# W1 in two pieces behind its first three groups, and new engine orders for the middle blocks

## The chip, the cores and the metric

The kernel runs on one core of one Trainium2 chip. The metric is the device time of one execution in microseconds (us). The time before is the median of three runs, 292.15 us (291.99 to 292.51).

## The reference, cut to what matters

All inputs are float32. Eight batches of eight heads, 576 rows, head width 64; then 4608 tokens of width 512 through a two-layer network with 2048 hidden columns.

```python
def _attn_ref(q, k, v):
    q_s = np.exp(q - np.max(q, axis=-1, keepdims=True))
    q_s = q_s / (np.sum(q_s, axis=-1, keepdims=True) + 1e-09)
    k_s = np.exp(k - np.max(k, axis=2, keepdims=True))
    k_s = k_s / (np.sum(k_s, axis=2, keepdims=True) + 1e-09)
    kv = np.einsum('bhsd,bhse->bhde', k_s, v)
    return np.einsum('bhsd,bhde->bhse', q_s, kv)

def _moe_ref(x, w_in, w_out):
    h = x @ w_in
    g = np.where(h > 0.0, h, np.exp(np.minimum(h, 0.0)) - 1.0)
    return g @ w_out
# x is the attention's result, transposed to tokens x 512
```

## The kernel before, in words

**Tiles.** The network runs over nine blocks of 512 tokens, called j = 0 to 8. In a block the 2048 hidden columns are eight groups g = 0 to 7 of 256 columns. A group takes eight matmuls of 128x512 on PE (`hg_mm`, L622) into one PSUM buffer of 1024 columns. ACT takes the exponential (L672), for most groups ACT then takes 1 minus it, cut at zero (L674), and DVE joins both with the product into the tile GR (L678, two halves). Only when DVE has read the buffer may PE use it again, which is two groups later. The second layer is `out_mm` (L699) for blocks 0 and 1. From block 2 on it is `pair` (L832), seven products in the place of eight; these need sums of parts of GR (`add_sum`, L783, on DVE or POOL) and of parts of the weights W2 (`combos`, L759), and DVE adds up the results (L841).

**Attention beside it.** Sixteen half batches n = 0 to 15 are worked on between the groups of earlier blocks. Each loads Q, K and V (L361), takes exponentials on ACT (L397, L401), row sums on DVE (L423, L425), scales Q (L435, on DVE or POOL) and casts V (L279). From n = 4 on a DMA transpose on SP's queue (L472) turns the scaled Q into QT, and `widen` (L279) copies it to qsT. PE takes K times V (L509); DVE makes MBLK out of it (L518, L522); PE multiplies with qsT (L540), and `xt` copies the result into XT (L279), the input of the first layer.

**Order.** Nothing is scheduled at run time. `program` adds some 1400 operations, numbered in the order in which they are added; `ORDER` lists, for each of the five engines, which of them it runs and in which order. An operation with several possible engines (`alts`) goes to the one whose list holds its number. `emit` puts a semaphore wait ahead of an operation where something that it needs runs on another engine or is a DMA. Each engine works through its list in order, and so an operation that waits holds up all that stand behind it on its engine. `AFTER` adds four waits by hand.

**Loads of W1.** POOL issues them (`load_w1`, L379). Columns of groups 0 to 2 come first in four parts (operations 14 to 17, 384 KB each), then group 3, group 4, group 5 (18, 19, 20; 512 KB each), then groups 6 and 7 (21; 1024 KB). POOL's list begins `1 32 14 15 24 16 17 18 48 40 19 20 21 69 68 70`: 48 scales Q, 40 casts V, both for half batch 1, and 69, 68 and 70 are loads of W2 and Q. PE reaches groups 3, 4, 5, 7, 6 of block 0 in this order (operations 99, 103, 110, 133, 121). The wait for a load stands ahead of a group's first weight load (PEld).

**Operations named below**, by their numbers of before:

- 318: scaling of Q for n = 7 (L435). 355: copy of a finished output tile (L279). 241: a copy into XT (L279). 360 (ACT, L674), 361 and 362 (DVE, L678): block 2, group 3. 370: first layer of block 2, group 5, which waits for 362; ahead of it on PE stands 313 (L540).
- 671 (DVE, L841) and 672 (PE, L832): one partial result in block 3's second layer.
- 564 and 565 (ACT), 566 and 567 (DVE): block 3, group 7 with its first-layer product 563. 579 (DVE, L678): block 4, group 0, second half; 645: first layer of block 4, group 2, which waits for 579.
- 219, 230, 236: loads of K (n = 6), Q and V (n = 7) on SP's queue. 180, 181, 183, 184, 186, 187, 189, 190: the eight stores of block 0 (L728). 238: the cast of V on POOL that waits for load 236. 393: a sum of W2 parts on POOL. 240: PE's products that wait for 238 (L540, L509).

Of the kernel before, what the change touches and what calls it, by code (L numbers as in the profile page):

```python
# [24 lines left out]
ISSUE = {"sp": 550, "act": 550, "gp": 740}  # L25
ORDER = {
# [24 lines left out]
    "act": (  # L51
# [12 lines left out]
    "dve": (  # L64
# [37 lines left out]
}  # L102

APART = ((1, 1), (1, 2))
AFTER = ((209, 197), (228, 261), (235, 275), (307, 288))


class Op:
    __slots__ = ("eng", "dur", "emit", "deps", "key", "idx", "start", "end",
# [167 lines left out]
class Gen:  # L277
# [610 lines left out]
    def program(self):  # L888
# [8 lines left out]
        self.load_w1(0, 3, (0,), -30, [gate])  # L897
        for kc in range(1, 4):
            self.load_w1(0, 3, (kc,), -30)
        for g0, g1 in ((3, 4), (4, 5), (5, 6), (6, 8)):  # L900
            self.load_w1(g0, g1, range(4), -30)
        AB, C, D_ = 3, 2, 1
        self.stage1(0, -8, vconv=CAST0)
# [174 lines left out]
            one[i]()  # L1078
            two[i]()
        for a, b in AFTER:  # L1080
            S.ops[a].deps.setdefault(S.ops[b], "raw")


S_ = S
# [32 lines left out]
```

## Time and profile before

| | us |
|---|---|
| median of three runs (lowest, highest) | 292.15 (291.99, 292.51) |
| time of the profiled execution | 292.0 |
| its span in the trace | 290.2 |
| time outside of the span | 1.8 |
| busy: PE, DVE, ACT, POOL | 280.1, 231.5, 212.1, 160.3 |
| DMA, mean over the span | 172 GB/s |

The span runs from the first to the last instruction that the trace holds. Busy times are sums over instructions; matmuls overlap, and so a busy PE need not be a PE without gaps. The chain of waits is followed back from the last instruction, and where the chain stays on PE, PE had work at hand.

### The profile page before, as it was taken

What the parts mean: (1) busy time and instruction counts of PE and PEld (TensorE: products, weight loads), DVE (VectorE), ACT (ScalarE), POOL (GpSimd) and SP (SyncE); (2) the same over time, 40 slices, a digit from 0 to 9 for tenths busy, and PEclk for the clock granted to TensorE, in tenths of its full rate; (3) what the DMA queues carried; (4) which work ended last, traced back from release to release, by engine and by line L of the source; (5) the groups of instructions that cost most, each with busy time, mean ns of one, the idle gap of its engine ahead of it and who ended that gap; (6) DMA issues with size and microseconds to landing.
All of it is one profiled execution on the core that took longest, in us unless ns stands there. A gap on an engine that the chain in (4) does not pass through costs nothing.

```text
span 290.2 us, 5483 instructions
## 1 busy us (share of the span) xinstructions
PE 280.1 (97%) x2176; PEld 243.7 (84%) x2176; DVE 231.5 (80%) x432; ACT 212.1 (73%) x237; POOL 160.3 (55%) x159
## 2 busy tenths in 40 slices
PE   2899999999999999999999999999999999999995
PEld 0488887888888899989899998989999999989995
DVE  3758847886699998898998879797785978668884
ACT  4858838989999877989887788857687546655510
POOL 1992443426356679409776793845417712794441
PEclk9999999999999999999999999999999999999999
DMA  7999999897989724775686457322211001400244
GB/s 260 395 369 388 390 388 357 219 212 253 267 246 292 209 103 111 248 189 172 133 267 198 122 82 277 69 48 52 63 36 38 0 2 30 114 0 20 56 97 123
DMA packets 36474, 50.04 MB, mean 172 GB/s; under 512 B 16352, under 2 KB 18144, under 8 KB 36448
## 3 DMA queue, kind: packets, MB, share of 16 engines
q1 hardware_dynamic: 29680, 33.96, 42.6%
q0 software_dynamic: 6528, 15.47, 17.6%
q8 instruction: 17, 0.28, 0.4%
q10 hardware_dynamic: 240, 0.26, 0.3%
q14 instruction: 9, 0.07, 0.1%
HBM read 36.70 MB, written 9.44 MB: 159 GB/s over the span
## 4 chain that ended last, share of the span: by engine, by line
PE 91%; DVE 3%; DMA 2%; POOL 2%; ACT 0%; SPq 0%; issue 0%
PE PS L622 44%; PE PS L832 32%; PE PS L699 9%; PE PS L540 3%; DMA KR<-in_k_dram 2%; PE PS L509 2%; DVE GR L678 1%; POOL W L379 1%; DVE QS L435 0%; DVE ZQ L423 0%; POOL VB L279 0%; PE PS L459 0%; POOL QS L435 0%; DVE MBLK L522 0%; ACT GE L674 0%; SPq L361 0%
## 5 line engine op out<-in xcount | busy, mean ns | idle before, releaser
L622 PE MATMUL PS<-XT,W 128*128 128x512 f32 x576 | 141.5, 393 | 0.1
L622 PEld LDWEIGHTS PS<-XT,W 128*128 128x128 f32 x576 | 105.3, 188 | 21.1 <-DVE GR L678 0.3
L678 DVE SCALAR_TENSOR_TENSOR GR<-PS,GE 128x512 fp32r<-128x512 f32 x112 | 76.7, 686 | 20.6 <-ACT GE L674 19.2
L672 ACT ACTIVATE GE<-PS 128x1024 f32<-128x1024 f32 x56 | 57.4, 1024 | 43.1 <-PE PS L622 36.2
L783 POOL TENSOR_TENSOR GR<-GR 128x256 fp32r<-128x256 f32 (+1 forms) x50 | 48.5, 981 | 47.7 <-DVE SB L783 29.0
L674 ACT ACTIVATE GE<-GE 128x1024 f32<-128x1024 f32 x56 | 59.4, 1060 | 1.5
L832 PE MATMUL PS<-TB,GR 128*128 128x256 f32 x336 | 52.5, 283 | 0.0
L832 PE MATMUL PS<-W,GR 128*128 128x256 f32 x336 | 52.2, 283 | 0.0
L832 PEld LDWEIGHTS PS<-TB,GR 128*128 128x128 f32 x336 | 46.5, 191 | 1.4 <-DVE OSB L841 0.3
L832 PEld LDWEIGHTS PS<-W,GR 128*128 128x128 f32 x336 | 46.5, 191 | 1.1
L435 POOL TENSOR_TENSOR QS<-QR,RZQ 128x1152 f16<-128x1152 f32 (+1 forms) x15 | 27.7, 1845 | 29.5 <-DVE RZQ L425 26.2
L841 DVE TENSOR_TENSOR OSB<-OSB,PS 128x256 f32<-128x256 f32 x84 | 34.8, 416 | 10.8 <-PE PS L832 9.3
L699 PE MATMUL PS<-W,GR 128*128 128x512 f32 x128 | 32.2, 394 | 0.0
L783 POOL TENSOR_TENSOR GR<-SB,GR 128x256 fp32r<-128x256 f32 (+1 forms) x26 | 25.4, 985 | 8.2 <-PE PS L832 7.4
L699 PEld LDWEIGHTS PS<-W,GR 128*128 128x128 f32 x128 | 23.6, 188 | 4.5
L423 DVE TENSOR_REDUCE ZQ<-QR 128x18 f32<-128x1152 f32 (+2 forms) x18 | 21.7, 1208 | 5.8 <-ACT QR L421 4.9
L783 POOL TENSOR_TENSOR SB<-GR 128x256 fp32r<-128x256 f32 (+1 forms) x19 | 18.6, 981 | 11.8 <-PE PS L832 7.1
L401 ACT ACTIVATE KR<-KR 128x1152 bf16<-128x1152 f32 x16 | 18.4, 1158 | 2.7 <-DMA KR<-in_k_dram 2.7
L783 DVE TENSOR_TENSOR GR<-GR 128x256 fp32r<-128x256 f32 (+1 forms) x34 | 19.9, 595 | 0.1
L397 ACT ACTIVATE QR<-QR 128x1152 f32<-128x1152 f32 x14 | 16.2, 1158 | 1.8 <-DMA QR<-in_q_dram 1.7
L279 POOL CAST VB<-VR 128x1152 bf16<-128x1152 f32 (+1 forms) x11 | 12.2, 1111 | 8.6 <-DMA VR<-in_v_dram 8.6
L832 PE MATMUL PS<-W,SB 128*128 128x256 f32 x104 | 16.8, 283 | 0.0
(67 smaller groups left out, 265.1 us busy)
## 6 DMA issues: line engine op xcount, KB each, us to landing
out_dram<-OSB SPq DMA_DIRECT2D x61, 128.0 KB, 2.4
QR<-in_q_dram SPq DMA_DIRECT2D x12, 576.0 KB, 5.4
KR<-in_k_dram SPq DMA_DIRECT2D x12, 576.0 KB, 5.4
VR<-in_v_dram SPq DMA_DIRECT2D x12, 576.0 KB, 5.7
W<-in_moe_w_out_dram POOLq DMA_DIRECT2D x4, 1024.0 KB, 16.3
QR<-in_q_dram POOLq DMA_DIRECT2D x4, 576.0 KB, 11.9
VR<-in_v_dram POOLq DMA_DIRECT2D x4, 576.0 KB, 13.0
KR<-in_k_dram POOLq DMA_DIRECT2D x4, 576.0 KB, 14.0
```

The source lines that it names most:

```text
L397: S.add("act", t_act(1152, False), lambda e: e.activation(flat(q), flat(q), AF.Exp), key - 3, X=[f"qR{i}0", f"qR{i}1"])
L401: S.add("act", t_act(1152, False), lambda e: e.activation(ek[:, :, :, :].rearrange("p h c d -> p (h c d)"), flat(k), AF.Exp), key - 2, X=[ ...
L423: S.add("dve", t_dve(m), lambda e, qp=qp, zp=zp: e.tensor_reduce(zp, qp, AX.X, ALU.add), key - 3, R=[f"qR{i}{x}" for x in xs], W=[f"ZQ{i}{ ...
L435: lambda e, qp=q[:, :, a:b, :], rz=rz, dst=qs[:, :, a:b, :]: e.tensor_tensor(dst, qp, rz, ALU.mult),
L622: last = e.matmul(P[:, t * 512:(t + 1) * 512], self.W1[:, kc, tt * 128:(tt + 1) * 128], self.XT[:, kc, rc:rc + BLK], start=(kc == 0), stop ...
L672: S.add("act", t_act(1024, True), lambda e: e.activation(ge, P, AF.Exp), key, W=own, X=banks)
L674: S.add("act", t_act(1024, False), lambda e: e.activation(ge, ge, AF.Relu, bias=1.0, scale=-1.0), key, X=own)
L678: S.add("dve", t_dve(512 if j else 1024), lambda e, u=u: e.scalar_tensor_tensor(*(x[:, :, u, :] if j else x for x in (gt, P)), 0.0, ge[:, ...
L699: last = e.matmul(dst, self.tile(jb, jj, ts), self.W2[:, jj, c0:c1], start=(jj == 0), stop=(jj == 15))
L783: lambda e: e.tensor_tensor(dst, a, b, op), key, R=R, W=W, X=X, after=after)
L832: last = e.matmul(dst, a[i][:, y_, :], b[i][:, y_, :], start=start and i == 0 and y_ == 0, stop=stop and i == len(grps) - 1 and y_ == z - ...
L841: S.add("dve", t_dve(256), lambda e: e.tensor_tensor(dst, a, b, ALU.add), key, R=R, W=W, X=X, after=after)
```

## The change

The loads of W1 behind the first three groups become two: groups 3 and 4 (1024 KB), and groups 5 to 7 (1536 KB). There are two operations fewer, and so every number from 22 on is two lower in the lists of after. The lists of all five engines are given anew. Apart from the two loads that are gone and from SP's stores (below), they differ from the last second-layer products of block 1 (about 69 us in the trace of before) to the middle of block 6 (about 212 us), and neither ahead of that nor behind it. `AFTER` names the same four pairs of operations under their new numbers, and writes the wait in where `setdefault` left one of another kind as it was; none of the four pairs had one.

```diff
-        for g0, g1 in ((3, 4), (4, 5), (5, 6), (6, 8)):
+        for g0, g1 in ((3, 5), (5, 8)):
             self.load_w1(g0, g1, range(4), -30)
...
-AFTER = ((209, 197), (228, 261), (235, 275), (307, 288))
+AFTER = ((207, 195), (226, 259), (233, 273), (305, 286))
...
         for a, b in AFTER:
-            S.ops[a].deps.setdefault(S.ops[b], "raw")
+            S.ops[a].deps[S.ops[b]] = "raw"
...
     "gp": (
-        "1 32 14 15 24 16 17 18 48 40 19 20 21 69 68 70 73 72 71 74 75 76 77 120 131 116 143 144 "
+        "1 30 14 15 22 16 17 18 46 38 19 67 66 68 71 70 69 72 73 74 75 118 129 114 141 142 161 130 "
...
     "sp": (
-        "8 9 10 11 12 13 205 207 210 220 229 219 180 230 236 309 308 190 183 356 184 347 239 181 "
-        "249 357 189 319 187 248 326 186 348 320 418 392 377 391 329 378 338 419 494 495 511 510 "
+        "8 9 10 11 12 13 203 205 208 218 227 185 187 181 179 217 178 188 228 182 234 307 306 355 "
+        "184 237 354 345 247 317 324 346 246 376 318 389 416 390 375 336 327 417 492 493 337 427 "
...
     "dve": (
-        "275 276 222 282 283 305 288 306 289 295 296 355 302 303 316 343 242 344 243 317 244 318 "
-        "245 352 246 353 247 415 361 362 394 395 416 314 367 368 405 373 323 374 376 402 407 403 "
+        "273 274 220 280 281 303 304 286 287 293 294 300 301 314 315 239 240 341 342 241 242 243 "
+        "413 350 244 245 351 359 414 360 403 365 366 374 393 371 372 405 400 406 397 380 381 460 "
...
-        "582 552 536 537 556 562 568 539 540 545 628 541 546 630 572 566 567 616 617 621 442 443 "
-        "592 578 444 579 654 655 445 650 637 446 638 593 659 665 447 671 648 649 642 747 675 697 "
+        "543 566 544 538 539 570 564 590 439 615 626 440 630 565 441 442 576 652 577 653 443 629 "
+        "444 591 635 657 445 636 663 646 669 745 647 673 586 667 588 695 668 679 696 694 680 746 "
```

Read with the numbers of before, the new lists do this:

- 73 operations change their engine: 24 go from DVE to POOL (19 sums of GR, 4 sums of W2, the scaling 318), 19 sums of GR from POOL to DVE, 14 copies from DVE to ACT (355 among them), 6 copies from ACT to DVE (241 among them), 8 copies and casts from ACT to POOL, 2 casts from POOL to ACT. PE's 457 operations, DMAs left aside, stay the same.
- SP issues 187, 189, 183 and 181 right behind the transpose 229 and ahead of load 219, 190 ahead of load 230, and 184 ahead of load 236 (180 stood ahead of 230 before).
- POOL runs 393 ahead of 238; before, it ran 238 first.
- DVE's list from 566 to 579 is 566, 592, 441, 617, 628, 442, 632, 567, 443, 444, 578, 654, 579. ACT's list has 564 right behind 433, with no exponential of K (437) between.

125 rows, old and new, of the table ORDER are left out of this document.

## The prediction

> **What bounds the kernel now.** I read first the span and PE's clock, then busy times, then what PE waited for, then the chain of waits.
>
> ```profile
> core 0: 290.2 us, clock 0.999
> PE 280.1 (97%) x2176; PEld 243.7 (84%) x2176; DVE 231.5 (80%) x432; ACT 212.1 (73%) x237; POOL 160.3 (55%) x159
> PE PS L918 <- ACT QR L421: 5.7, 1, 5.7
> ```
>
> The third row is the longest of PE's waits by far, and it is the start: PE waits for the first Q. The chain, in order of time, shows the rest.
>
> ```profile
> 14.44 1.58 PE PS L622 x6
> ...
> 16.49 13.20 PE PS L622 x58
> ...
> 75.75 0.20 PE PS L540 x2
> ...
> 76.87 0.49 ACT XT L279
> ...
> 80.48 1.37 DVE QS L435
> ...
> 83.77 1.35 DVE ZQ L423
> ...
> 85.88 0.70 DVE GR L678
> ...
> 86.63 2.08 PE PS L622 x8
> ...
> 125.40 1.66 PE PS L832 x14
> ...
> 135.00 1.84 PE PS L622 x8
> ...
> 271.46 15.37 PE PS L832 x128
> 286.85 0.42 DVE OSB L841
> ```
>
> From 14.44 us PE carries the chain to 286.85, but for one stretch from 76.87 to 86.63. Between lies PE's own work at full clock: 272.4 us. Neither its 457 operations nor the lists ahead of 69 us (PE's) and behind 212 us change. The change can take away only what PE waits between 14.4 and 286.9, and that is little; it can add as much as the new lists hold PE up. So there is much more room above the time than below it.
>
> The one stretch off PE, closer (instructions in order of time):
>
> ```profile
> 83.42 1.06 ACT L674 ACTIVATE GE<-GE 128x1024 f32<-128x1024 f32 x1
> ...
> 86.13 0.40 PE L540 MATMUL PS<-qsT,MBLK 128*128 128x256 f32 x2
> ...
> 86.63 1.66 PEld L622 LDWEIGHTS PS<-XT,W 128*128 128x128 f32 x8 [0.31 <-DVE GR L678]
> ```
>
> PE's weight load for 370 stood idle for 0.31 us until DVE had read the buffer (362, the chain's 85.88 row). That is what the new lists can win here: 0.3 us. The short gaps at changes between kinds of product stay, since their products do.
>
> **The change part by part.** *The wait at 86.3 us.* 361 could have started when ACT's 360 ended, 83.42 + 1.06 = 84.48. It started only behind a row sum that ended at 83.77 + 1.35 = 85.12. Ahead of it DVE loses 318 (1.37) and the copy 355 (512 columns, priced at the 0.69 of L678's 512, row below), and gains 241 (384 columns, under 0.69; I take 0.5): 1.5 us less. So 361 starts at 84.5. With a reciprocal now between, at half of 0.69, 362 ends at 84.5 + 0.69 + 0.35 + 0.69 = 86.2, and PE comes to 370 at 86.63 - 0.31 = 86.3. The wait goes, by a hair: -0.3 us. POOL takes 318 and ACT takes 355; POOL has 45% of the span free, and ACT loses 241 (0.49) to DVE just there.
>
> *W1 in two pieces.* The POOL issues, their way to landing, the weight loads on PE and the rate of all DMAs:
>
> ```profile
> 10.87 1.39 POOL L379 DMA_DIRECT2D W<-in_moe_w_in_dram  x2
> ...
> 13.71 0.82 POOL L379 DMA_DIRECT2D W<-in_moe_w_in_dram  x1
> ...
> 14.52 1.47 POOL L379 DMA_DIRECT2D W<-in_moe_w_in_dram  x2
> ...
> W<-in_moe_w_in_dram POOLq DMA_DIRECT2D x1, 384.0 KB, 5.6
> ...
> W<-in_moe_w_in_dram POOLq DMA_DIRECT2D x1, 512.0 KB, 6.7
> ...
> W<-in_moe_w_in_dram POOLq DMA_DIRECT2D x1, 1024.0 KB, 9.4
> ...
> 20.23 0.19 PEld L622 LDWEIGHTS PS<-XT,W 128*128 128x128 f32 x1
> ...
> 23.63 0.41 PEld L622 LDWEIGHTS PS<-XT,W 128*128 128x128 f32 x2
> ...
> 11.50:15.00 3.50, 2.69 (x48) 1.46 (x47) 2.52 (x9) 2.65 (x4) 3.50 (x6) 1.00 1.22 402
> 15.00:20.00 5.00, 5.00 (x23) 4.07 (x22) 1.54 (x3) 2.21 (x3) 5.00 (x8) 1.00 1.69 358
> 20.00:25.00 5.00, 5.00 (x24) 4.13 (x23) 4.58 (x6) 4.67 (x6) 3.43 (x5) 1.00 1.42 385
> ```
>
> The last of the four early parts is issued at 10.87 and lands 5.6 later, at 16.5. Group 4's piece (13.71 + 6.7) lands at 20.4, groups 6 and 7 (issued in the last row at 14.52 + 0.73 = 15.25, + 9.4) at 24.6. PE's first weight load of group 3 is at 20.23, that of group 5 two groups later at 23.63 + 0.22 = 23.85. Now group 3 must wait for what was group 4's landing, and group 5 for what was that of groups 6 and 7. The DMA engines are never idle here (last figure of the windows, GB/s): 402 where rows of 3 KB come in, 358 with 1 KB rows, 385 with 2 KB rows. The new pieces have 2 KB and 3 KB rows. The first, 1.05 MB, gains 2.93 - 2.72 = 0.2 and lands at 20.2, in time within 0.1. The second, 1.57 MB at 402, takes 3.9 and lands at 24.1: PE stops for group 5 for 24.1 - 23.85 = 0.25, with the semaphore 0.3 us. Bounds: with the bytes no faster than now it lands at 24.6, 0.8 us; with the rate steady from 16.5 on (2.62 MB in 6.6 us, 23.1), 0. I take +0.3. Behind 30 us no PE wait of the trace could swallow it. POOL's two issues fewer (0.74 each) start the loads behind them 1.5 us earlier; since the engines are full this gives those loads the 0.5 us that the rates give, and no product waits for them: 0.
>
> [...]
>
> *The other lists.* 73 operations change engine. Prices:
>
> ```profile
> L678 DVE SCALAR_TENSOR_TENSOR GR<-PS,GE 128x512 fp32r<-128x512 f32 x112 | 76.7, 686 | 20.6 <-ACT GE L674 19.2
> ...
> L672 ACT ACTIVATE GE<-PS 128x1024 f32<-128x1024 f32 x56 | 57.4, 1024 | 43.1 <-PE PS L622 36.2 <-PE PS L832 6.8
> ...
> L783 POOL TENSOR_TENSOR GR<-GR 128x256 fp32r<-128x256 f32 x33 | 26.1, 796 | 29.8 <-DVE SB L783 20.0 <-PE PS L832 9.6
> ...
> L783 DVE TENSOR_TENSOR GR<-GR 128x256 fp32r<-128x256 f32 x23 | 12.5, 554 | 0.1
> ```
>
> A sum of 256 columns costs POOL 0.80 and DVE 0.55. Five operations more leave DVE for POOL than come back, 14 copies go to ACT and 6 come: DVE becomes shorter, and most new places have room. I followed the lists; DVE is closest to PE at 645, which waits for 579. PE leaves 563 at about 125.4 + 0.1; ACT's 564 and 565 (1.02 + 1.06) follow at once and end at 127.6. Then DVE has 13 operations: four halves of L678 (2.74), a row sum (1.35), a sum of 512 columns (628, as 0.69), two of 256 (617 and 632, 1.1) and the copy 441 (0.55), together 6.4; and four short ones, between nothing and 0.55 each. It ends between 134.0 and 136.2, and PE begins 645 at 135.0. So between no wait and 1.2 us; the middle, 135.1, costs 0.1, which I take.
>
> *SP's stores* wait for nothing new, but stand ahead of three loads (rivals). The new `AFTER` puts in the same four waits: 0.
>
> The sum goes against the profiled execution: 290.2 of span and 1.8 outside of it, 292.0, which is 0.15 below the median of 292.15 and inside the three runs. 292.0 - 0.3 + 0.3 + 0.1 = **292.1 us**. This is no change: I count under 0.2% (0.6 us), about the spread of the three runs, as what a measurement can't tell from none.
>
> **The rivals.** *All waits go (faster).* W1's second piece lands at 23.1 to 23.8, 645 finds 579 done, 370's wait goes: 292.0 - 0.3 = 291.7. POOL's issue ahead of PE's start may be shorter with 2 KB rows (0.82 for a lone one of 1 KB rows against 1.47 / 2 for the last two), 0.1, and some tenths of shorter waits inside PE's stretches may go as well: 291.4. For it: longer rows move faster in the windows. Against: group 4's landing at 20.4, 3.9 us behind the early parts for 1.05 MB that take 2.9 at 358; this 1 us of lag the new pieces inherit.
>
> *A V load late (slower).* SP's queue, the landing of load 236 in its window, and POOL:
>
> ```profile
> 62.08 1.31 SPq L361 DMA_DIRECT2D KR<-in_k_dram  x1
> 63.44 0.55 SPq L728 DMA_DIRECT2D out_dram<-OSBX  x1
> ...
> 65.39 0.37 SPq L361 DMA_DIRECT2D VR<-in_v_dram  x1
> ...
> VR<-in_v_dram SPq DMA_DIRECT2D x1, 576.0 KB, 5.9
> ...
> 68.31 2.12 POOL L435 TENSOR_TENSOR QS<-QR,RZQ 128x1152 f16<-128x1152 f32 x1 [0.90 <-DVE RZQ L425]
> 71.37 1.15 POOL L279 CAST VB<-VR 128x1152 bf16<-128x1152 f32 x1 [0.94 <-DMA VR<-in_v_dram]
> ...
> 82.80 2.41 POOL L759 TENSOR_TENSOR TB<-W 128x1024 fp32r<-128x1024 f32 x1
> ```
>
> Six stores more stand between the transpose and load 236: at 0.6 each 3.6 us of issue, of which 0.8 was free; it goes out 2.8 later, at 68.2, and lands at 74.1 in the place of 71.3. POOL now runs 393 (2.41) first, to 72.9, waits, and ends the cast at 74.1 + 1.15 = 75.25; PE wants it at 75.75. From a landing at 74.6 on each us later stops PE, and with it the cast's followers on POOL. If the stores' own 0.8 MB slow the queue by another 1 to 1.5 us, PE loses 0.5 to 1.0: 292.6 to 293.1, say 292.9.
>
> *DVE and POOL in each other's way (slower).* 0.55 is the mean of DVE's sums beside a busy POOL. If POOL's added work makes DVE's four operations in SBUF ahead of 579 (592, 617, 628, 632) longer by 0.25 each, 645 waits 1.0 more: 293.1. For it: the lists put POOL's longest sums where DVE is full. Against: DVE also loses work. [...]
>
> *The lists don't do it.* 370's wait stays, since the reciprocal and ACT's new copy use up the hair: 292.4, no change.
>
> **How the numbers follow.** Forecast 0.38 (291.6 to 292.7, same); all waits go 0.23, of it 0.17 beyond 0.2% and 0.06 within; V load 0.15 and DVE against POOL 0.18, both slower; the lists don't do it 0.06, same. Faster 0.17, same 0.38 + 0.06 + 0.06 = 0.50, slower 0.33. The range for 8 in 10 takes in the faster case down to 291.4 and the slower ones up to 293.2.
>
> **What would show it.** Right: the chain from 14.4 us is all PE, without the ACT and DVE rows between 77 and 86; the weight load of group 5 in block 0 comes at 24.1 to 24.2 with an idle time for a DMA of W; cast 238 ends ahead of 75.6; PE's last row starts where now 286.85 stands, within 0.3. Wrong: an idle PE weight load for VB near 76 (V load), or for GR near 105, 135 or 142 (DVE); or no idle time at 24 us at all.

## The result and the profile after

| | before | after |
|---|---|---|
| median of eight executions each (us) | 292.31 | 293.46 |
| lowest, highest (us) | 291.99, 293.06 | 292.83, 294.87 |
| profiled execution, its span (us) | 292.0, 290.2 | 294.87, 293.1 |

The changed kernel is slower by 0.4%, 1.2 us: ratio 1.0041, 95% interval 1.0021 to 1.0061. The prediction had 292.1 us and a range up to 293.2. The profiled execution of after is the longest of its eight, so its waits are at their long end; the experiments below say what each costs at the median.

The span, the busy times and what PE and its weight load waited for, in the trace of after (waits: us in total, times, longest; those that before has too, or that lie ahead of PE's steady run at 14 us, are left out):

```profile
core 0: 293.1 us, clock 0.999
```
```profile
PE 280.6 (96%) x2176; PEld 243.4 (83%) x2176; DVE 228.4 (78%) x419; ACT 209.6 (72%) x239; POOL 173.4 (59%) x168
```
```profile
PE PS L621 <- DVE GR L677: 1.0, 1, 1.0
PE PS L539 <- POOL VB L278: 0.9, 1, 0.9
...
PE PS L621 <- DMA W<-in_moe_w_in_dram: 0.5, 1, 0.5
...
PEld PS L539 <- POOL VB L278: 1.3, 1, 1.3
...
PEld PS L621 <- DVE GR L677: 1.2, 1, 1.2
...
PEld PS L621 <- DMA W<-in_moe_w_in_dram: 0.9, 1, 0.9
```

PE's busy time is that of before within 0.5 us. Three waits are new: 2.4 us by PE's rows, 3.4 by those of its weight load, which runs ahead of PE (a product begins 0.12 us behind the start of its weight load, median in after). Less the 0.3 us of the wait that went, these are 2.1 and 3.1 us; the 2.9 us by which the span grew lie between the two. The chain of waits has the same three places, where before it had only the stretch from 76.87 to 86.63:

```profile
13.65 11.14 DMA W<-in_moe_w_in_dram
24.83 5.76 PE PS L621 x24
...
69.61 6.73 DMA VR<-in_v_dram
76.40 1.16 POOL VB L278
...
198.31 2.31 DVE SB L782
200.65 0.70 DVE GR L677
201.37 0.70 DVE GR L677
202.12 2.11 PE PS L621 x8
...
274.33 15.36 PE PS L831 x128
```

Between 78 and 192 us all its pieces are PE's. The last row started at 271.46 before: 2.87 us late. In time order (timeline of after):

```profile
24.83 0.76 PEld L621 LDWEIGHTS PS<-XT,W 128*128 128x128 f32 x4 [0.93 <-DMA W<-in_moe_w_in_dram]
...
61.14 2.38 SPq L471 DMA_TRANSPOSE QT<-QS  x1
63.56 2.95 SPq L727 DMA_DIRECT2D out_dram<-OSBX  x4
66.55 0.60 SPq L360 DMA_DIRECT2D KR<-in_k_dram  x1
67.19 1.14 SPq L727 DMA_DIRECT2D out_dram<-OSBX  x2
68.37 0.59 SPq L360 DMA_DIRECT2D QR<-in_q_dram  x1
69.00 0.57 SPq L727 DMA_DIRECT2D out_dram<-OSBX  x1
69.61 0.59 SPq L360 DMA_DIRECT2D VR<-in_v_dram  x1
...
76.40 1.15 POOL L278 CAST VB<-VR 128x1152 bf16<-128x1152 f32 x1 [2.82 <-DMA VR<-in_v_dram]
...
77.60 0.30 PEld L539 LDWEIGHTS PS<-qsT,MBLK 128*128 128x128 f32 x2 [1.35 <-POOL VB L278]
...
88.37 1.01 PEld L621 LDWEIGHTS PS<-XT,W 128*128 128x128 f32 x5
...
198.20 2.13 POOL L434 TENSOR_TENSOR QS<-QR,RZQ 128x1152 f16<-128x1152 f32 x1
...
198.31 2.31 DVE L782 TENSOR_TENSOR SB<-GR 128x256 fp32r<-128x256 f32 x1
...
200.65 1.42 DVE L677 SCALAR_TENSOR_TENSOR GR<-PS,GE 128x512 fp32r<-128x512 f32 x2
...
202.12 1.69 PEld L621 LDWEIGHTS PS<-XT,W 128*128 128x128 f32 x8 [1.17 <-DVE GR L677]
```

Three stories. At 24 us the second W1 piece is late. At 77 us the load of V goes out behind seven stores (at 65.39 before), lands at 69.61 + 6.73 = 76.34, and PE waits for its cast. At 202 us PE waits for DVE, whose sum of 256 columns took 2.31 us: it began 0.11 us behind a POOL instruction and ended 0.29 us behind that one's end (198.20 + 2.13 = 200.33). The weight load at 88.37 has no idle time: the wait of before at 86.63 is gone.

### The profile page after: what moved, and what is told of

Same layout as the page of the kernel before. It is cut to its first block, busy times and chain, and to the rows that moved or that the text cites. A ratio compares the mean times of both kernels' runs of the same rounds, so it can differ in the third digit from the quotient of the medians.

```text
span 293.1 us, 5465 instructions
## 1 busy us (share of the span) xinstructions
PE 280.6 (96%) x2176; PEld 243.4 (83%) x2176; DVE 228.4 (78%) x419; ACT 209.6 (72%) x239; POOL 173.4 (59%) x168
## 4 chain that ended last, share of the span: by engine, by line
PE 84%; DMA 8%; DVE 3%; POOL 2%; ACT 1%; issue 0%; SPq 0%
PE PS L621 40%; PE PS L831 30%; PE PS L698 9%; DMA W<-in_moe_w_in_dram 4%; PE PS L539 3%; DMA VR<-in_v_dram 2%; DMA KR<-in_k_dram 2%; PE PS L508 2%; POOL W L378 1%; DVE GR L677 1%; DVE SB L782 1%; POOL VB L278 1%; DVE OSB L840 0%; PE PS L458 0%; POOL QS L434 0%; ACT GE L673 0%
## 5 line engine op out<-in xcount | busy, mean ns | idle before, releaser
L782 POOL TENSOR_TENSOR GR<-GR 128x256 fp32r<-128x256 f32 (+1 forms) x47 | 45.1, 968 | 35.5 <-DVE SB L782 25.3
L434 POOL TENSOR_TENSOR QS<-QR,RZQ 128x1152 f16<-128x1152 f32 (+1 forms) x16 | 30.6, 1910 | 23.5 <-DVE RZQ L424 21.4
L782 POOL TENSOR_TENSOR GR<-SB,GR 128x256 fp32r<-128x256 f32 (+1 forms) x26 | 24.5, 948 | 18.1 <-DVE GR L782 9.0
L782 POOL TENSOR_TENSOR SB<-GR 128x256 fp32r<-128x256 f32 (+1 forms) x22 | 21.4, 977 | 7.5 <-DVE GR L677 6.5
L782 DVE TENSOR_TENSOR GR<-GR 128x256 fp32r<-128x256 f32 (+1 forms) x37 | 21.3, 587 | 0.1
L278 ACT ACTIVATE OSB<-PS 128x256 f32<-128x256 f32 (+1 forms) x24 | 9.7, 407 | 15.4 <-PE PS L831 14.2
L278 ACT ACTIVATE XT<-PS 128x640 fp32r<-128x640 f32 (+6 forms) x22 | 12.8, 586 | 6.8 <-PE PS L539 3.7
L671 ACT ACTIVATE ESB<-PS 128x1024 f32<-128x1024 f32 x14 | 14.1, 1026 | 4.5 <-PE PS L621 4.1
```

The costliest lines, as they stand in the source:

```text
L278: return e.activation(dst, src, AF.Copy) if e is self.nc.scalar else e.tensor_copy(dst, src)
L434: lambda e, qp=q[:, :, a:b, :], rz=rz, dst=qs[:, :, a:b, :]: e.tensor_tensor(dst, qp, rz, ALU.mult),
L671: S.add("act", t_act(1024, True), lambda e: e.activation(ge, P, AF.Exp), key, W=own, X=banks)
L782: lambda e: e.tensor_tensor(dst, a, b, op), key, R=R, W=W, X=X, after=after)
```

## The experiments

Theory A, from the profile of after: the time goes at the three places above, each by its own mechanism (a larger W1 piece, six stores ahead of a load, a DVE sum beside POOL). The rivals are that one part is all of it, or that the new lists cost time everywhere. Theories B and C came up on the way and are told where they are tried. Each row has 5 to 12 executions. All ratios are against the kernel before on the same chip in the same comparison, where its median was 292.17 to 292.33; a ratio is taken over all these executions and can differ a little from the ratio of the two medians. Times of two rows of the table come in part from different chips. Edits are to the changed kernel unless "before" is said. **Numbers of operations**: 760, 821, 822, 920 and 948 to 959 are those of the changed kernel (two lower than before's); all others below are those of before, where the expectation of best_two does not say otherwise.

| kernel | lowest, median, highest (us) | ratio, 95% interval |
|---|---|---|
| w1_only | 292.30, 292.50, 293.08 | 1.0010, 1.0002 to 1.0019 |
| lists_only | 292.55, 293.51, 293.99 | 1.0038, 1.0024 to 1.0052 |
| sp_as_before | 292.62, 292.78, 294.88 | 1.0027, 1.0014 to 1.0039 |
| sum_later | 292.13, 293.06, 295.57 | 1.0031, 1.0013 to 1.0049 |
| split_scale | 291.93, 292.80, 293.39 | 1.0009, 0.9998 to 1.0020 |
| stores_only | 292.01, 292.72, 293.76 | 1.0015, 1.0004 to 1.0025 |
| mended_two | 291.77, 292.20, 293.94 | 1.0001, 0.9988 to 1.0013 |
| mended_four | 291.86, 292.49, 294.59 | 1.0023, 1.0004 to 1.0042 |
| cast_later | 292.09, 293.14, 295.26 | 1.0034, 1.0017 to 1.0052 |
| load_later | 291.55, 292.47, 293.78 | 1.0005, 0.9992 to 1.0017 |
| best_two | 292.79, 293.87, 295.78 | 1.0060, 1.0039 to 1.0081 |
| best_four | 292.11, 294.06, 295.00 | 1.0051, 1.0033 to 1.0070 |
| copy_behind | 292.21, 292.69, 293.39 | 1.0012, 1.0003 to 1.0021 |
| copy_early | 295.41, 296.63, 296.75 | 1.0137, 1.0119 to 1.0155 |
| all_four | 292.35, 293.27, 294.46 | 1.0035, 1.0021 to 1.0049 |
| all_two | 292.13, 293.30, 294.48 | 1.0032, 1.0021 to 1.0044 |
| final_four | 291.31, 291.92, 293.78 | 0.9996, 0.9979 to 1.0012 |
| final_two | 291.35, 292.59, 294.07 | 1.0012, 0.9996 to 1.0028 |

### W1 alone, and the lists alone

```diff
 w1_only (before, its own lists, renumbered)      lists_only (after, its own lists, renumbered)
-((3, 4), (4, 5), (5, 6), (6, 8))                -((3, 5), (5, 8))
+((3, 5), (5, 8))                                +((3, 4), (4, 5), (5, 6), (6, 8))
```

> The kernel before with W1 in two pieces; its lists stay, renumbered. Theory A (the changed kernel loses time at three places: the second W1 piece, the V load, and a DVE sum held up by POOL): PE stands 0.7 to 0.8 us idle at 23.9 us for the second piece, which lands at 24.6 to 24.7, and nothing later makes up for it: 0.7 us over before. Rival 1 (the prediction's term): the piece lands at 24.1, 0.3 us over before. Rival 2 (the lists are all of it): no idle time, the time of before within 0.2.

> The changed kernel with W1 in four pieces as before; the new lists stay. Theory A: nothing waits at 24 us; PE still waits for the cast of V near 75.5, 0.9 to 1.2 us; the wait of 0.37 us at 86.3 is gone; and near 200 us PE waits 0 to 1.2 us for GR, by whether POOL's scaling of Q starts ahead of DVE's sum 952 (0.1 us lay between the two starts). In all 0.6 to 1.8 us over before, and some 0.7 under the changed kernel. Rival 2 (the lists are all of it, W1 nothing): the time of the changed kernel. Rival 3 (W1 is all of it): 0.4 under before.

w1_only costs 0.1%, 0.3 us (0.1 to 0.6). In its trace the second piece is nearly in time (its weight load in the timeline):

```profile
24.04 1.46 PEld L627 LDWEIGHTS PS<-XT,W 128*128 128x128 f32 x7 [0.21 <-DMA W<-in_moe_w_in_dram]
```

So rival 1, the prediction's own term, is right in size at the median, and the 0.93 us of after's trace is one long case of the wait. In this trace itself the wait cost PE little: set against the same matmuls of before, those behind the landing come only 0.08 us later than those ahead of it (0.8 us in after), and so the trace does not show that the 0.3 us is this wait. The lists cost 1.1 us (0.38% of 292.23; 0.7 to 1.5). lists_only has the other two waits of after, and a new one, for a load of W2:

```profile
PE PS L626 <- DVE GR L682: 0.9, 1, 0.9
PE PS L544 <- POOL VB L283: 0.5, 1, 0.5
...
PE PS L703 <- DMA W<-in_moe_w_out_dram: 0.2, 1, 0.2
```

lists_only was expected 0.7 us under the changed kernel and is level with it (293.51 and 293.46), as rival 2 had it. The wait for W2 is a part of that. With four pieces of W1, PE's weight load waits 0.2 to 0.8 us for W2 near 32 us in six of the eleven traces on record (0.60 here); with two pieces, where POOL issues these loads 1.5 us earlier (the first at 14.45 in w1_only, 15.98 in before), it does so in none of nine. Two pieces thus lose time at 24 us and can win some at 32.

### The stores ahead of the V load

```diff
 sp_as_before
-... 218 227 185 187 181 179 217 178 188 228 182 234 307 306 355 ...
+... 218 227 217 178 228 234 307 306 185 187 181 179 188 182 355 ...
 stores_only (before)
-... 229 219 180 230 236 309 308 190 183 356 184 347 239 181 249 357 189 319 187 ...
+... 229 187 189 183 181 219 180 190 230 184 236 309 308 356 347 239 249 357 319 ...
```

(sp_as_before is written in the changed kernel's numbers.)

> The changed kernel with the six stores of block 0 put back behind the loads of K, Q and V on SP's list. Theory A: the V load goes out 3 to 4 us earlier, POOL's cast ends ahead of PE's need, no PE wait near 76; 1.0 us under the changed kernel (0.9 to 1.2). Rival 4 (the V load is late for another reason: the DMA transpose ahead of it, or the W1 pieces, which delay everything by 0.8): the wait stays at 0.8 or more, and the time is that of the changed kernel.

> The kernel before with one part of the change alone: SP issues 187, 189, 183, 181 behind the transpose 229, 190 ahead of load 230 and 184 ahead of load 236, as the new list does. Theory A: the V load goes out about 3.5 us later, the cast on POOL ends 0.3 to 1.0 us behind PE's need at 75.7, PE waits that long near 75.7; 0.3 to 1.0 us over before. POOL's long sum 393 stays behind the cast here, so the cast's 1.15 us starts as soon as the load lands. Rival 4 (the stores do not matter, the V load is late only with the other new lists): no wait, the time of before.

With the stores back the V load goes out at 65.62, the cast ends at 73.94, and PE's wait near 76 is gone; the median is 0.7 us under the changed kernel's, where 1.0 was expected; the intervals of the two ratios overlap. The stores alone, in the kernel before, cost 0.15%, 0.4 us (0.1 to 0.7), with this row in the timeline:

```profile
76.00 0.30 PEld L545 LDWEIGHTS PS<-qsT,MBLK 128*128 128x128 f32 x2 [0.62 <-POOL VB L284]
```

The load goes out at 68.83 and lands at 74.75, both 3.4 us later than before. Rival 4 falls: no other part of the lists is needed for this wait.

### The DVE sum beside POOL

```diff
 sum_later, DVE
-... 952 948 949 ...
+... 948 949 952 ...
 split_scale: POOL's 920, one instruction of nine chunks
-(0, 9)
+(0, 5), then (5, 9)
```

> The changed kernel with DVE's sum 952 moved behind 948 and 949, the two operations that free PE's buffer. Theory A (952, two inputs in SBUF, is held up until POOL's scaling of Q ends, 2.3 us for 0.42): 948 starts as soon as ACT is done, and PE's wait for GR near 201 us (1.2 us) is gone; 952 takes its long time behind them, where PE does not wait. The time is 0 to 1.2 us under the changed kernel, by how many of its executions had the wait. Rival 5 (DVE simply has too much work there, whatever POOL does): only the 0.42 us of the sum is won, and PE still waits 0.7 us or more.

> The changed kernel with one edit: POOL's scaling of Q 920 (2.13 us, the one beside DVE's sum 952) is issued as two instructions of 5 and 4 chunks (about 1.2 and 1.0 us); the same work, all lists the same. Theory A (a DVE sum with its data in SBUF is held up until the POOL instruction in flight has ended): 952 ends about 0.3 us behind the first half, so it takes 1.3 to 1.6 us in the place of 2.31, and PE's wait for GR near 200 us falls from 1.1 to 0.1 to 0.4 us; the time falls 0.7 to 1.0 under the changed kernel's. Rival 5 (DVE is late there for lack of time): PE's wait stays at 1.1 and the time stays. Rival 6 (DVE is held up for as long as POOL works, whatever the size of its instructions): 952 stays at 2.3.

split_scale changes nothing but the length of two POOL instructions. Its timeline:

```profile
196.94 2.46 POOL L441 TENSOR_TENSOR QS<-QR,RZQ 128x640 f16<-128x640 f32 x2
...
197.04 1.45 DVE L791 TENSOR_TENSOR SB<-GR 128x256 fp32r<-128x256 f32 x1
...
200.00 1.68 PEld L630 LDWEIGHTS PS<-XT,W 128*128 128x128 f32 x8 [0.31 <-DVE GR L686]
```

The sum falls from 2.31 to 1.45 us: it ends 0.28 us behind the first half (1.27 us long in the trace), though POOL goes on working. That is theory A and neither rival 5 nor rival 6. PE's wait falls from 1.17 to 0.31, and the median by 0.7 us, the low end of what was expected; of the repairs tried one by one this is the only one whose interval (0.9998 to 1.0020) lies apart from the changed kernel's. In sum_later PE does not wait for GR at all there, which rival 5 excluded; but its weight load waited 0.59 us for DVE's adding up at 202, since 952 then stood beside the next POOL sum (1.21 us), and 0.84 us at 177, where DVE's copy 849 had waited 1.4 us for a store. Its median is only 0.4 us down.

### Mending the three places

```diff
 mended_two: sp_as_before and sum_later together, and on SP
-... 822 760 821 ...
+... 822 821 760 ...
 mended_four: the same, with W1 in four pieces
```

> The changed kernel with the three places in the lists mended (the six stores behind the loads, 952 behind 949, and one store, 821, ahead of the Q load 760 on SP, whose landing DVE had waited for near 177 us), and W1 still in two pieces. Theory A: of the 1.2 us that the change cost, the lists' part of about 1.0 goes, and the 0.37 us at 86.3 stays won: 0.1 under to 0.3 over before (292.1 to 292.5), with PE idle 0 to 0.7 us at 23.9. Rival 7 (the new lists cost time all over): 0.6 or more over before.

> The same three places mended, and W1 in four pieces as before. Theory A: 0.2 to 0.4 us under before, 291.8 to 292.0, from the wait at 86.3 us that is gone; 0.2 to 0.4 us under the version with W1 in two pieces. Rival 7: 0.3 or more over before.

mended_two is level with before: all of the 1.2 us is won back at the median. The parts measured alone fit this: 0.3 for W1, 0.4 for the stores and 0.7 for the sum, less the 0.3 us of the wait that went, are 1.1, each known to some 0.3 us. mended_four should have been 0.3 under before and was not: four of its twelve executions lay at 293.7 to 294.6. The standard deviation of before in these comparisons is 0.22 to 0.30 us, that of w1_only 0.20; of the versions with the new lists 0.4 to 0.9, and of stores_only, which has the lists of before but for the stores, 0.5. The lists cost not only at fixed places, they make the time spread, and the stores ahead of loads already do so by themselves.

### Looking for the spread

```diff
 cast_later: mended_four, ACT               load_later: mended_four, SP
-... 600 604 700 701 ...                    -... 602 677 676 596 ...
+... 600 700 701 604 ...                    +... 677 676 602 596 ...
 best_two, best_four: mended, cast_later's move, 952 behind 959,
 SP's stores of block 0 all in before's places (348 goes out later by that)
```

> The version with three places mended and four W1 pieces, and one more edit: on ACT the cast 604, which waits for the load 602 of V and stood 0.8 us idle for it at 148.8, goes behind 700 and 701. Theory B (a third of the executions of the new lists lose another 1.5 us and more because ACT stands behind a late V load there, with 1.0 us to spare for PE): the median falls to 291.9 to 292.2, and no execution is over 293.2. Rival 8 (the late executions come from elsewhere): the median stays at 292.5 and some executions stay at 294.

> The same version with 604 where the new list has it, and the load 602 of V moved behind two stores on SP, so that it goes out about 1.2 us later. Theory B (1.0 us to spare): ACT stands idle 2.0 to 2.6 us at 149 and PE waits 0.2 to 1.5 us near 154.5 for GR; the profiled time rises by that much, and the median to 292.7 to 294. Rival 8: the time of the version without this edit, PE does not wait there.

> The changed kernel, W1 in two pieces, with all places mended: SP's first part in the order of before, store 821 ahead of load 760, cast 602 (new number) behind 699 on ACT, DVE's sum 952 behind 959. Theory A: no PE wait over 0.2 us but the one for W1 at 24 us (0 to 0.7): 291.8 to 292.3, that is 0 to 0.4 under before. Rival 7 (the new lists cost time in many places): over 292.5.

> The same with W1 in four pieces. Theory A: the 0.37 us at 86.3 is won and nothing is lost: 291.7 to 292.0, 0.2 to 0.5 under before. Rival 7: over 292.3.

Theory B was that ACT's wait for V near 149 us makes the long executions. With the cast out of the way (cast_later) no time was won. load_later does not test the other side: SP stands idle ahead of this load in mended_four (from 140.65 to 144.61), and the two stores fell into that idle time. The load went out at 144.49 and landed at 148.31, no later than in mended_four (148.77). best_two and best_four were the worst so far, but the profiles of cast_later, best_two and best_four fell on long executions and showed the same place. Timeline of best_four:

```profile
92.58 0.69 DVE L283 COPY OSB<-PS 128x512 f32<-128x512 f32 x1 [1.32 <-PE PS L703]
93.19 1.76 DVE L763 TENSOR_TENSOR TB<-W 128x1024 fp32r<-128x1024 f32 x1
94.88 1.41 DVE L682 SCALAR_TENSOR_TENSOR GR<-PS,GE 128x512 fp32r<-128x512 f32 x2
...
96.33 1.68 PEld L626 LDWEIGHTS PS<-XT,W 128*128 128x128 f32 x8 [1.99 <-DVE GR L682]
...
164.08 0.38 ACT L283 ACTIVATE OSB<-PS 128x256 f32<-128x256 f32 x1 [3.06 <-DMA out_dram<-OSB]
...
164.51 0.53 PEld L836 LDWEIGHTS PS<-W,GR 128*128 128x128 f32 x4 [0.95 <-ACT OSB L283]
```

The first row is the copy 376. The row names PE, but 376 also waits for store 348 to leave its buffer, and that landed at 92.50 (88.9 in load_later, whose copy ran at 90.83). Behind it stands the W2 sum 395, 1.76 us beside POOL instead of 1.22, and only then 373 and 374, which free PE's buffer. In the list of before 395 stands far ahead and 376 behind 374. In cast_later the copy was in time, but ACT had waited 1.6 us for a load of K, and 395 took 2.19 us: the same wait of PE's weight load, 1.9 us. At 164 us the copy 784 waited for store 724, which took 7.2 us to land behind a Q load (3.8 in load_later).

### The copy ahead of PE's buffer

```diff
 copy_behind: mended_four, DVE              copy_early (before), DVE
-... 367 368 376 395 373 374 ...            -... 394 395 ... 405 373 323 374 376 ...
+... 367 368 373 374 376 395 ...            +... 394 ... 405 376 395 373 323 374 ...
 all_four, all_two: copy_behind, 604 behind 701, 784 on DVE behind 733, 952 behind 959
```

> The version with three places mended and four W1 pieces, and on DVE the copy 376 and the W2 sum 395 put behind 373 and 374. Theory C (that order is the cause of the long executions): no PE wait over 0.2 us between 90 and 100 us, no execution over 293.2, median 291.9 to 292.2. Rival 8 (the long executions come from elsewhere): median 292.5, some executions at 294.

> The kernel before with this one change: DVE runs 376 and 395 ahead of 373. Theory C: the copy waits for the store 348 (landed at 91.1 in the trace of before) and 395 takes 1.2 to 2.2 us; DVE then comes to 373 and 374 1.5 to 3 us later than before, PE waits 0.5 to 2 us near 95 us, median 0.5 to 2 over before, and the executions spread over 1 us or more. Rival 8: the time of before within 0.3.

> The same as the first, and besides the cast 604 behind 701 on ACT, the copy 784 back on DVE behind 733, the sum 952 behind 959. Theory C: 291.7 to 292.0, every execution under 292.8. Rival 7 (the new lists cost time in many places): over 292.3.

> The same with W1 in two pieces. Theory C: 0.1 to 0.4 us more than with four pieces, 291.9 to 292.3, with a PE wait of 0 to 0.7 us at 24 us. Rival: no more than with four pieces (within 0.1), if PE has the time to spare behind 24 us.

Theory C is that the order of 376 and 395 ahead of 373 and 374 makes the long executions. copy_behind took the longest away (highest 293.39, standard deviation 0.37 instead of 0.92), nearly as theory C has it (no more than 293.2), but the median did not fall: DVE came 1.9 us later to what follows than in load_later, and PE's weight load waits 0.56, 0.75 and 0.53 us at 92, 95 and 100, where no wait over 0.2 was expected. copy_early shows how dear the order can be, though not by the wait that was expected: in before's order PE runs 375, whose result 376 copies, two products later, and the copy waited for that. Timeline, and windows with PEclk as the figure ahead of the last two:

```profile
93.49 1.81 DVE L764 TENSOR_TENSOR TB<-W 128x1024 fp32r<-128x1024 f32 x1
...
97.29 1.45 PEld L627 LDWEIGHTS PS<-XT,W 128*128 128x128 f32 x7 [3.06 <-DVE GR L683]
```
```profile
95.00:100.00 5.00, 2.71 (x10) 0.88 0.70 184
100.00:105.00 5.00, 5.00 (x94) 0.78 0.13 15
105.00:110.00 5.00, 5.00 (x33) 1.00 0.72 226
```

PE stood still for 2.6 us (3.1 by its weight load), and then ran at a granted clock of 0.88 over 95 to 100 us, 0.78 over 100 to 105, and 1.00 again behind that; over the ten us the missing clock adds up to 1.7 us. Together that is 4.3 us, by which this execution (296.54) lies over before's median (292.28), a miss of the 0.5 to 2 us that were expected. all_four and all_two were worse than copy_behind: in the trace of all_four 784, now on DVE, stood 1.31 us idle for the same late store 724, and PE's weight load 0.86 for it; theory C, by which all_four was expected at 291.7 to 292.0, does not cover this place. In these traces a copy that waits for a store holds up whichever engine it is on: ACT for 3.06 us in best_four, DVE for 1.31 in all_four.

### Each wait taken out

```diff
 final_four: mended_four, and on DVE 952 behind 959, and
 DVE                                        SP
-... 405 367 368 376 395 373 374 ...       -... 751 723 724 ...
+... 405 395 367 368 373 374 376 ...       +... 723 724 751 ...
 final_two: final_four, with W1 in two pieces
```

> The version with three places mended and four W1 pieces, and DVE's sum 395 ahead of 367 (DVE stood idle there from 87.3 to 89.6 us), its copy 376 behind 374, its sum 952 behind 959, and on SP the Q load 751 behind the stores 723 and 724. Theory C (the waits found are all that the new lists cost): no PE wait over 0.2 us but those of before, 291.6 to 292.0, no execution over 292.8. Rival 7 (behind each wait stands another that shows once it is gone): 292.3 or more, and a wait of PE of 0.3 us or more at a new place.

> The same with W1 in two pieces. Theory C: 0 to 0.7 us of wait at 24 us, 0.1 to 0.4 over the version with four: 291.8 to 292.3. Rival 7 as there.

The trace of final_four has no new wait of PE; these are all that it lists, and the span is 0.6 us under before's:

```profile
PE PS L922 <- ACT QR L425: 5.5, 1, 5.5
PE PS L556 <- DVE MBLK L526: 0.5, 1, 0.5
PE PS L513 <- POOL VB L283: 0.2, 1, 0.2
```
```profile
core 0: 289.6 us, clock 1.000
```

Five of its twelve executions took 291.31 to 291.40; the lowest of before's 23 was 291.83. But others took up to 293.78, and the median is not told apart from before's. So the new lists can be 0.5 us faster where nothing is late, and they are not faster as a rule. final_two is 0.7 us over it at the median, more than w1_only's 0.3, and the intervals overlap. What lengthens the other executions of the final versions isn't known: both profiles fell on short ones. That it is again a late transfer is likely from the others, and not shown. Some long executions had a lower clock: the longest of sum_later (295.57 us) had a mean granted clock of 0.994 and four of the five of copy_early 0.992 to 0.994, while every other execution in the table had 0.997 to 1.000.

## Why the prediction was wrong

**W1, +0.3: right in size, in part by luck.** It put the pieces' landings at 20.2 and 24.1; w1_only had 20.1 and 24.0, and cost 0.3. Group 5 started right behind the landing of the whole piece in both traces: at 24.04 behind 24.0 in w1_only, at 24.83 behind 24.79 in after. But the term took idle time of the weight load, which runs ahead of PE, for time that PE loses: 0.21 us of it cost PE 0.08 in w1_only. What PE's matmuls lose at the two landings goes from 0.02 (final_two) to 1.3 us (best_two) in the nine traces with two pieces, and the upper bound, a landing at 24.6, was passed in after's trace (24.8). Against it stands what the prediction put at 0, "no product waits for them": with four pieces PE's weight load waits for W2 in six of eleven traces.

**The wait at 86.3, -0.3: right.** It is gone in after, for the reason given, and in the trace of final_four, where nothing else delays PE.

**"The other lists", +0.1: this is the step that failed.** It measured 1.1 us (0.7 to 1.5) in lists_only. The wait that the step priced, 645 for 579, did not come (the chain at 135 us is PE's). The step walked the lists with one duration for each kind of operation, took what came closest, and so had no term for what doesn't depend on the operation itself:

- *Transfers.* "SP's stores wait for nothing new", and their price, 0.5 to 1.0 us, was put in a rival with a chance of 0.15. The rival's working was nearly right: 74.1 for the landing, 74.75 in stores_only, because the load went out 3.4 us later and not 2.8. It should have been a term of the sum: its own threshold (74.6) was half a microsecond from its estimate.
- *A sum beside POOL.* The rival had the two engines in each other's way, but spread it as 0.25 us, a supposition that no run shows, on four operations ahead of 579. It comes whole, on one instruction, where a POOL instruction has just begun: 1.9 us on 952. The timeline of before has a case:

```profile
89.22 2.12 POOL L435 TENSOR_TENSOR QS<-QR,RZQ 128x1152 f16<-128x1152 f32 x1 [4.00 <-DVE RZQ L425]
...
90.92 0.97 DVE L783 TENSOR_TENSOR SB<-GR 128x512 fp32r<-128x512 f32 x1
```

  POOL ends at 91.34 and the sum at 91.89, 0.97 us for what takes 0.68 elsewhere. The mean of 0.55 in the grouped row hid this: it mixes 0.42 with cases of 0.7 to 1.5.
- *Copies that wait for stores.* Not in the prediction at all. They don't lengthen every execution, they spread the time (standard deviation 0.92 us in mended_four, 0.37 in copy_behind).

**"DVE becomes shorter, and most new places have room"**: DVE's busy time did fall, 231.5 to 228.4, and POOL's rose by 13.1. It was no argument: what counted was which instruction stood beside which.

**The range** ended at 293.2 because each slower rival was priced alone. In lists_only and in after two of them came together.

## What to carry to other kernels

When a hand-made order is changed, look in each engine's list for operations that wait for a DMA and count what stands behind them: a load behind stores, or a copy that waits for a store, ahead of the operation that frees PE's buffer, costs by how late the transfer happens to be, and shows as spread before it shows in a median (here a standard deviation of 0.5 us in stores_only and 0.92 in mended_four, at medians 0.4 and 0.2 over before, which has 0.22 to 0.30). Price a two-input DVE sum by its slowest case beside POOL (2.31 us here), not by its mean (0.55). One profile shows one execution; profiles of several variants found the place at 95 us that the profile of after didn't show.

## What the runs showed of the hardware

**DVE beside POOL.** In the traces of before and after 20 DVE sums of 256 columns with both inputs in SBUF began while POOL had more than 0.4 us of an instruction left: they took 0.72 to 2.31 us, and every one of them ended 0.28 to 0.29 us behind POOL's instruction. The 57 that began beside no POOL instruction took 0.41 to 0.43. Of L678's 128x512 kind, with one input in PSUM, 104 began beside POOL in the same way and took 0.69 us in the mean, as did the 91 that began beside none. In split_scale, where POOL's instruction was two, the sum ended 0.28 us behind the first of them. In load_later the order is the other way round: DVE's 395 began first (1.22 us from 91.43), and POOL's sum of W2 parts that began beside it at 92.17 took 1.62 us instead of 1.30.

**The clock after a wait.** In copy_early PE was idle for 2.63 us up to 97.29, its weight load for 3.06, and the granted clock was 0.88 over 95 to 100, 0.78 over 100 to 105 and 1.00 from 105 us on; six products of 128x256 took 1.48 us from 99.60 and 0.88 from 107.47. The one execution of copy_early whose mean clock stayed at 1.000 took 295.41 us, the other four (0.992 to 0.994) 296.54 to 296.75. best_four's execution with waits of 1.7 to 2.0 us had a mean clock of 1.000.
